# Three pairs of chunks by seven block products in place of two, in a linear-attention and three-gate kernel

## The chip, the cores and the metric

The kernel runs on one core of a Trainium2 chip. The metric is the device time of one execution in microseconds (us), lower is better. TensorE (PE) multiplies matrices and loads its stationary operand by a separate sequence (PEld); VectorE (DVE), ScalarE (ACT) and GpSimd (POOL) work elementwise; SyncE (SP) issues most of the data transfers (DMAs). Each engine works through its instructions in the order in which the program has them, and waits for others by semaphores.

## The reference

Linear attention over batch 8, 8 heads, 576 positions, head size 64, and behind it a layer of three gates whose maximum is taken:

```python
q_s = softmax(q, axis=-1)              # over the 64 of a head
k_s = softmax(k, axis=2)               # over the 576 positions
kv  = einsum('bhsd,bhse->bhde', k_s, v)
x   = einsum('bhsd,bhde->bhse', q_s, kv).transpose(0, 2, 1, 3).reshape(4608, 512)
h   = max(x @ w1, x @ w2, x @ w3)      # 4608 x 768
out = h @ w_out                        # 4608 x 512
```

All inputs of the attention are 32-bit floats; the weights arrive as 64-bit floats. The result is wanted at 32-bit accuracy.

## The kernel before

**Precision.** TensorE's fast format (float32r) doesn't hold a whole 32-bit float. Each operand of a large product is therefore split into a high and a low part, and a product of two blocks is three matmuls: low x high, high x low, high x high. A matmul has 128 x 128 stationary and 128 x 512 moving elements.

**Weights.** The three gate weights come in 18 slices of 512 KB (slice n = 3j+i is weight i, columns 128j to 128j+127), w_out in 6. For each slice VectorE and ScalarE shift, clamp and mask the two words of the 64-bit number (L402 to L411), GpSimd adds them (L415), ScalarE makes the high part (L423) and VectorE or GpSimd the low one (L430). The parts stay on chip as `wh`, `wl` (gates) and `oh`, `ol` (w_out).

**Chunks.** The 4608 rows of x make nine chunks of 512: chunk c < 8 is the first 512 rows of batch c; chunk 8 is the 64 rows left over in each of the 8 batches. Attention runs per batch and pair of heads (n = 4b + g): batches 0 and 1 in a form of their own at the start ("turned"; `q` is their query tile, worked on by ScalarE where n is in `Q_BY_ACT`, L675, otherwise by VectorE and ScalarE, L680 to L701), batches 2 to 7 with the rows of `qt` (max, subtract, exp, sum, scale: L688 to L707; transpose to `tb`, L712; eight small DMAs to `qT`, L725; high and low part, L734 and L737). The product with kv leaves x in PSUM (L799), from which x is split (L807 to L819) for a direct chunk, or copied to `xf` (L822, L824) for a paired one.

**Direct gates.** Chunks 0 to 4: for each of 6 blocks of columns and 3 weights, 4 blocks of the inner dimension x 3 products, 216 matmuls (L894); the maxima go over ScalarE (L903) and VectorE (L906), h is split, and the second product takes 72 matmuls (L941).

**Paired gates.** From `PAIRED` on, two chunks are taken together (class `Duo`). The gate of two chunks is seen as a 2 x 2 block product and computed by seven block products P1 to P7 in place of eight (Strassen's scheme in Winograd's form). There are 9 units u (3 pairs of column blocks x 3 weights) of 7 products of 6 matmuls: 378 in place of 432 (L1103). The x operands `xb0` to `xb6` are made once per pair (L1049 to L1055), the weight blocks come from DRAM into small slots `ws` (L1082). Before the first pair, the stored weight blocks `wd` are prepared: three blocks of each unit are stored as they are, 54 stores of 128 KB (`prepare_weights`, L990), and four sums and differences are computed (`mix_weights`: VectorE adds high and low part, L1001, forms the blocks, L1007, ScalarE and VectorE split them, L1010 and L1013) and stored in two DMAs of 512 KB per unit. Before, the pairs are (5,6) and (7,8).

**Order.** All engines' orders are fixed when the program is built: each piece of work is a `Step` with an engine, a cost, conditions and a rank, and `Streams` places the steps by these. The constants at the top (`AT`, `CHUNK`, `LEFT_AT`, `FIRST_LOADS` and so on) are ranks. SyncE's queue issues in that order too; a DMA whose condition isn't met holds back those behind it. `xb` and `ws` lie where the gate weights lay, so they can't be written until the last direct gates have read them. A condition `before` in `Duo` says so:

```python
before = [("gates", PAIRED - 1), *(("kept", u) for u in range(9))] if c == PAIRED else [("gates", c - 2)]
```

Of the kernel before, what the change touches and what calls it, by code (L numbers as in the profile page):

```python
# [32 lines left out]
EAGER = 0.3  # L33

FIRST, CHUNK, SLICE = 143.0, 39.5, 1.32

AT = (38.7, -49.7, 32.6, 13.7, 143.7, 146.4, 163.0, 85.8)
STEP = (7.87, 0.38)
SLICES_AT, SLICE_STEP, SLICE_HI, SLICE_LO = -59.7, 0.11, 1.39, 0.51
GATES_AT = 1000.0  # L40
FIRST_LOADS = 'vkwkKqvwKVwVqqkwvqkv'
# [4 lines left out]
Q_BY_ACT = (0, 3, 4, 5, 6, 7)  # L46
# [162 lines left out]
def linear_attention_then_maxout_ffn(  # L209
# [133 lines left out]
    def by_f32(n):  # L343
        return X_F32 and n >= TURNED * NP
# [25 lines left out]
    class Slice:  # L370
# [25 lines left out]
        def join(self, room):  # L396
# [28 lines left out]
        def lo(self, room):  # L425
# [4 lines left out]
            unit[e].tensor_sub(out=lo, in0=self.view(self.low.bitcast(F32)), in1=h.bitcast(F32))  # L430
# [942 lines left out]
```

## Time and profile before

| what | value |
|---|---|
| median of 3 runs | 677.64 us (676.85 to 678.12) |
| profiled execution | 678.42 us |
| its span | 676.6 us |
| granted TensorE clock, mean | 0.992 |
| bytes moved by DMA | 107.64 MB |
| matmuls | 3434 |
| largest groups | L894 222.6 us, L1103 173.1 us, L941 59.7 us (one of several forms) |

The span runs from the first to the last recorded instruction; the execution's time is 1.82 us longer. A group's busy time is the sum of its instructions' times, which overlap on TensorE, so groups add to more than the engine's busy time. The profile's waits are idle time of an engine with what ended it.

### The profile page before, as it was taken

To read this page: it belongs to the slowest core of one execution; us is meant where nothing else is said; L and a number is where in the kernel's file an instruction comes from. 1 tells how busy PE (TensorE), PEld (TensorE's weight loads), DVE (VectorE), ACT (ScalarE), POOL (GpSimd) and SP (SyncE) were. 2 spreads that over 40 slices of the span, in tenths; PEclk is the share of its full clock that TensorE was granted. 3 is DMA by queue.
4 is the path that set the end of the run, shared out by engine and by line. 5 is a ranking of instruction groups with operands and counts; after the bars stand their busy time and mean duration, and the time that the engine had idled before them with its cause. 6 is when DMAs were issued, how large, how long until landed. Compare 5 with 4: busy or idle time off the path is not lost.

```text
span 676.6 us, 10151 instructions
## 1 busy us (share of the span) xinstructions
PE 646.9 (96%) x3434; PEld 530.3 (78%) x3434; DVE 463.5 (68%) x893; ACT 293.3 (43%) x660; POOL 61.4 (9%) x75
## 2 busy tenths in 40 slices
PE   2679999999999999999999999999999999999997
PEld 2467787788887888878888888888888788888875
DVE  5679998788707998899998998985525712333521
ACT  5579957433414443444444444644234432123132
POOL 2223232310100001101000001000000000000000
PEclk9979999999999999999999999999999999999999
DMA  9757634365755434554575646876665126766021
GB/s 231 193 159 235 168 95 141 115 173 145 221 173 156 122 89 145 159 179 125 143 211 169 177 132 204 267 221 173 204 191 166 63 89 193 190 197 195 24 63 62
DMA packets 125635, 107.64 MB, mean 159 GB/s; under 512 B 52368, under 2 KB 101008, under 8 KB 125584
## 3 DMA queue, kind: packets, MB, share of 16 engines
q1 hardware_dynamic: 125504, 106.87, 55.1%
q8 instruction: 27, 0.44, 0.3%
q14 instruction: 24, 0.20, 0.1%
q10 hardware_dynamic: 80, 0.13, 0.1%
HBM read 73.92 MB, written 25.95 MB: 148 GB/s over the span
## 4 chain that ended last, share of the span: by engine, by line
PE 87%; SPq 5%; DMA 4%; DVE 2%; issue 1%; ACT 1%; DVEq 0%; ACTq 0%
PE pf L894 34%; PE pf L1103 25%; PE pf L941 20%; DMA wst<-in_moe_w_dram 2%; PE pa L799 2%; PE pa L590 2%; PE sm L799 1%; DMA qt<-in_q_dram 1%; SPq L725 1%; DMA vt<-in_v_dram 1%; SPq L1224 1%; SPq L476 1%; PE sm L633 1%; DVE xb L1051 1%; SPq L1227 0%
## 5 line engine op out<-in xcount | busy, mean ns | idle before, releaser
L894 PE MATMUL pf<-x,wh 128*128 128x512 f32 x720 | 222.6, 390 | 0.0
L1103 PE MATMUL pf<-xb,ws 128*128 128x512 f32 x756 | 173.1, 389 | 0.0
L1103 PEld LDWEIGHTS pf<-xb,ws 128*128 128x128 f32 x756 | 141.6, 188 | 29.3
L894 PEld LDWEIGHTS pf<-x,wh 128*128 128x128 f32 x720 | 135.4, 188 | 27.5 <-issue 0.2
L894 PE MATMUL pf<-x,wl 128*128 128x512 f32 x360 | 143.8, 399 | 1.5 <-ACT m L903 0.9
L894 PEld LDWEIGHTS pf<-x,wl 128*128 128x128 f32 x360 | 67.7, 188 | 16.4 <-ACT m L903 1.3
L1132 DVE TENSOR_TENSOR mm<-pf,mm 128x512 f32<-128x512 f32 x24 | 16.6, 692 | 67.4 <-PE pf L1103 67.3
L941 PE MATMUL pf<-oh,hs 128*128 128x512 f32 x192 | 59.7, 390 | 1.0 <-DVE hs L1187 1.0
L906 DVE TENSOR_TENSOR m<-pf,m 128x512 f32<-128x512 f32 x60 | 41.3, 688 | 11.2 <-PE pf L894 10.4
L941 PE MATMUL pf<-ol,h_h 128*128 128x512 f32 x120 | 48.5, 404 | 0.0
L967 ACT COPY m<-pf 128x512 f32<-128x512 f32 x35 | 20.5, 587 | 63.5 <-PE pf L941 63.1
L560 POOL PARTITION_ALL_REDUCE kma<-km x24 | 21.3, 889 | 287.4 <-DVE km L557 218.1
L941 PE MATMUL pf<-oh,h_l 128*128 128x512 f32 x120 | 46.8, 390 | 0.0
L941 PE MATMUL pf<-oh,h_h 128*128 128x512 f32 x120 | 46.8, 390 | 0.0
L941 PEld LDWEIGHTS pf<-oh,hs 128*128 128x128 f32 x192 | 36.0, 188 | 9.3 <-DVE hs L1187 1.9
L415 POOL TENSOR_TENSOR wst<-wx,wst 128x512 int32<-128x512 int32 x24 | 31.8, 1327 | 87.7 <-DVE wx L411 64.7
L941 PE MATMUL pf<-ol,hs 128*128 128x512 f32 x96 | 37.6, 392 | 0.0
L1187 DVE TENSOR_TENSOR hs<-mm,hs 128x512 fp32r<-128x512 f32 (+1 forms) x32 | 16.7, 555 | 28.1 <-ACT hs L1185 28.1
L1151 ACT COPY pf<-pf 128x512 f32<-128x512 f32 x18 | 10.3, 570 | 57.7 <-PE pf L1103 57.7
L712 DVE STREAM_TRANSPOSE tb<-qt 128x576 f32<-128x576 f32 x24 | 30.6, 1276 | 1.7 <-DMA qT<-tb 1.0
L909 ACT CAST h_h<-m 128x512 fp32r<-128x512 f32 x30 | 18.6, 620 | 29.6 <-DVE m L906 29.6
L941 PEld LDWEIGHTS pf<-ol,h_h 128*128 128x128 f32 x120 | 22.5, 188 | 5.2 <-issue 0.7
(186 smaller groups left out, 936.5 us busy)
## 6 DMA issues: line engine op xcount, KB each, us to landing
ws<-wd SPq DMA_DIRECT2D x126, 256.0 KB, 3.0
wst<-in_moe_w_dram SPq DMA_DIRECT2D x18, 512.0 KB, 4.8
out_dram<-m SPq DMA_DIRECT2D x31, 256.0 KB, 2.8
vt<-in_v_dram SPq DMA_DIRECT2D x56, 128.0 KB, 3.0
qt<-in_q_dram SPq DMA_DIRECT2D x24, 288.0 KB, 3.5
qT<-tb SPq DMA_DIRECT2D x192, 36.0 KB, 1.9
kt<-in_k_dram SPq DMA_DIRECT2D x24, 256.0 KB, 3.2
wd<-mix_h SPq DMA_DIRECT2D x9, 512.0 KB, 3.2
```

The lines of the kernel that those rows point to most:

```text
L415: nc.gpsimd.tensor_add(out=low.bitcast(I32), in0=x.bitcast(I32), in1=low.bitcast(I32))
L560: nc.gpsimd.partition_all_reduce(kma, km, P, bass_isa.ReduceOp.max)
L712: nc.vector.transpose(out=tb.rearrange("p e (c s) -> p s e c", s=QS), in_=self.qt.rearrange("p s (e c) -> p s e c", e=2))
L799: nc.tensor.matmul(out=out, lhsT=l, rhs=r[:, cs], start=(i == 0), stop=(i == last))
L894: nc.tensor.matmul(out=ps, lhsT=l[:, cc, js], rhs=r, start=(cc == 0 and t == 0), stop=(cc == NC - 1 and t == 2))
L906: nc.vector.tensor_max(out=m, in0=self.m.pop((j, i)), in1=m)
L909: nc.scalar.copy(out=h, in_=m)
L941: nc.tensor.matmul(out=po, lhsT=l, rhs=r[:, j, :], start=(j == 0 and i == 0), stop=(j == NJ - 1 and i == 2))
L967: nc.scalar.copy(out=o, in_=po)
L1103: nc.tensor.matmul(out=bank[on], lhsT=w[:, a, k], rhs=x[:, b, k], start=(i == 0 and p in ("P1", "P5")), stop=(i == 5), skip_group_check=True,)
L1132: nc.vector.tensor_max(out=m, in0=bank[on], in1=m)
L1187: nc.vector.tensor_tensor(out=o[:, 1, jj], in0=mm[:, h, jj, ts], in1=o[:, 0, jj].bitcast(F32), op=ALU.subtract)
```

## The change

- `PAIRED` goes from 5 to 3: chunks 0 to 2 are direct, the pairs are (3,4), (5,6), (7,8). First-stage matmuls: 648 direct and 1134 paired in place of 1080 and 756.
- The high and low parts of the weights lie interleaved in `wa`. GpSimd's sum goes to one of four buffers `wf`, and each gate slice is stored from there as it is, as a plain float, to `keep_w` (18 stores of 256 KB during the start). `keep_weights` stores the split weights whole: 12 stores of 768 KB.
- `mix_weights` loads plain blocks from `keep_w` (9 loads of 512 KB) and no longer adds parts; one store of 1 MB per unit to `keep_s`.
- Weight loads of the pairs come from `keep_a` (P1, P4, P2: rows of 512 bytes) and `keep_s` (the other four products: 2 KB); 8 slots `ws` in place of 10; the buffers `s5`, `u2` are single.
- The x operands of the pairs are formed in another order, in place.
- Query work of batches 0 and 1 is on ScalarE for two pairs of heads (4 and 6) instead of six; exponentials of n = 8, 9 and scalings of n = 8 to 12 are done row by row on ScalarE; the main loads of v from batch 2 on are issued by ScalarE (48 DMAs); queries may be loaded earlier.
- The ranks are set anew.

Of the table of ranks two lines are shown.

```diff
-FIRST_LOADS = 'vkwkKqvwKVwVqqkwvqkv'
+FIRST_LOADS = 'vkwkKkqvwwKVVkqqqvwvk'
...
-Q_BY_ACT = (0, 3, 4, 5, 6, 7)
+Q_BY_ACT = (4, 6)
...
+NORM_FROM, NORM_TO = 8, 13
+ROWS_FROM, ROWS_TO = 8, 10
...
-PAIRED = 5
+PAIRED = 3
...
-    wh = [place(f"wh{i}", [P, NC, DF], F32R, W_AT + HALF * i) for i in range(3)]
-    wl = [place(f"wl{i}", [P, NC, DF], F32R, W_AT + HALF * (3 + i)) for i in range(3)]
+    wa = [place(f"wa{i}", [P, NC, 2, DF], F32R, W_AT + DF * NC * 8 * i) for i in range(3)]
+    wh, wl = ([t[:, :, hl, :] for t in wa] for hl in range(2))
...
+    wfs = Placed("wf", [P, CH], F32, SCR_AT, 4)
...
-    ws = [place(f"ws{i}", [P, 2, 2, P], F32R, SCR_AT + 2048 * i if i < 4 else W_AT + 57344 + 2048 * (i - 4)) for i in (0, 1, *range(4, 12))]
...
+    ws = [place(f"ws{i}", [P, 2, 2, P], F32R, W_AT + 57344 + 2048 * i) for i in range(8)]
...
-    wd = [dram.tile([P, 7, 2, 2, P], F32, name=f"wd{u}") for u in range(9)]
+    keep_a = [dram.tile([P, NC, 2, DF], F32, name=f"keep_a{i}") for i in range(3)]
+    keep_w = [dram.tile([P, 2, NC, P], F32, name=f"keep_w{u}") for u in range(9)]
+    keep_s = [dram.tile([P, 2, 2, 2, 2, P], F32, name=f"keep_s{u}") for u in range(9)]
...
+        def keep(self):
+            n = self.n
+            j, i = divmod(n, 3)
+            yield Step("S", 0.64, [("w", n)], gives=("plain", n), kb=256)
+            nc.sync.dma_start(out=keep_w[3 * (j // 2) + i][:, j % 2], in_=self.view(self.w))
...
+                    e = yield Step("S" if self.turned else V_ON, 0.64, [prev], kb=128 if self.turned else 200)
...
+                by_act = ROWS_FROM <= n < ROWS_TO
+                nc.vector.tensor_reduce(out=qm, in_=rows3, op=ALU.max, axis=AX.X, negate=by_act)
+                for s in range(QS if by_act else 0):
+                    if s % 3 == 0:
+                        yield Step("A", 3 * 0.33)
+                    nc.scalar.activation(
+                        out=rows3[:, s, :], in_=rows3[:, s, :], func=AF.Exp, bias=qm[:, s : s + 1],
+                        accum_out=qs[:, s : s + 1],
+                    )
+            if not self.turned and not by_act:
...
+            if NORM_FROM <= n < NORM_TO:
+                for s in range(QS):
+                    if s % 3 == 0:
+                        yield Step("A", 3 * 0.22, gives=("qn", n) if s == 6 else None)
+                    nc.scalar.activation(
+                        out=rows3[:, s, :], in_=rows3[:, s, :], func=AF.Copy, scale=qs[:, s : s + 1]
+                    )
...
-    WINO = {"P1": (0, 0), "P5": (6, 1), "P2": (1, 2), "P6": (3, 3), "P7": (5, 4), "P3": (4, 5), "P4": (2, 6)}
-
-    def prepare_weights():
-        for u in range(9):
-            jp, i = divmod(u, 3)
-            js = slice(2 * jp * P, 2 * (jp + 1) * P)
-            hv, lv = (t[i][:, :, js].rearrange("p c (r n) -> p r c n", r=2) for t in (wh, wl))
-            yield Step("S", 0.64, ["turn", ("split", 6 * jp + i), ("split", 6 * jp + 3 + i)], kb=128)
-            for part, (block, r, cc) in enumerate(((0, 0, 0), (1, 0, 2), (2, 1, 2))):
-                for hl, t in enumerate((hv, lv)):
-                    if part or hl:
-                        yield Step("S", 0.64, kb=128, gives=("kept", u) if part == 2 and hl else None)
-                    nc.sync.dma_start(out=wd[u][:, block, hl], in_=t[:, r, cc : cc + 2].bitcast(F32))
+    WINO = {
+        "P1": ("a", 0, 0), "P5": ("s", 1, 1), "P4": ("a", 1, 1), "P6": ("s", 0, 0), "P2": ("a", 0, 1), "P3": ("s", 0, 1),
+        "P7": ("s", 1, 0),
+    }
+    X_OF = {"P1": 0, "P5": 1, "P6": 2, "P2": 3, "P3": 4, "P7": 5, "P4": 6}
+
+    def keep_weights():
+        last = KEEP_AFTER
+        for i in range(3):
+            for c in range(NC):
+                e = yield Step(
+                    KEEP_ON, 0.64, [last, *(("split", 3 * j + i) for j in range(NJ))], gives=("kept", i, c), kb=768
+                )
+                (nc.sync if e == "S" else nc.scalar).dma_start(out=keep_a[i][:, c], in_=wa[i][:, c].bitcast(F32))
+                last = ("kept", i, c)
+            yield Step("-", 0.0, [last], gives=("kept", i))
...
-            for r in range(2):
-                yield Step("V", dve(CH), ["turn", "left", ("split", 6 * jp + i), ("split", 6 * jp + 3 + i)], port="V")
-                nc.vector.tensor_tensor(out=v[:, r], in0=hv[:, r].bitcast(F32), in1=lv[:, r].bitcast(F32), op=ALU.add)
+            yield Step("S", 0.64, ["left", ("plain", 6 * (u // 3) + u % 3), ("plain", 6 * (u // 3) + 3 + u % 3), ("low_mix", u - 1) if u else None], kb=512)
+            nc.sync.dma_start(out=v, in_=keep_w[u])
...
+            yield Step("S", 0.64, kb=1024, gives=("mixed", u))
+            nc.sync.dma_start(
+                out=keep_s[u].rearrange("p r c k t n -> p (r c k t n)"), in_=mix.rearrange("p r c t n -> p (r c t n)")
+            )
...
+                jp, i = divmod(u, 3)
+                kind, r, cc = WINO[p]
+                slot = ws[(at + n) % len(ws)].bitcast(F32)
+                after = [("kept", i) if kind == "a" else ("mixed", u)]
+                if c == PAIRED and n < len(ws):
+                    after.append(("gates", c - 1))
+                    after += [("kept", v) for v in range(3)]
                 yield Step("S", 0.64, after, take=[("ws", (c, p, u))], gives=("w", c, p, u), kb=256)
-                nc.sync.dma_start(out=ws[slot].bitcast(F32), in_=wd[u][:, WINO[p][0]])
+                if kind == "a":
+                    js = slice((2 * jp + r) * P, (2 * jp + r + 1) * P)
+                    nc.sync.dma_start(
+                        out=slot.rearrange("p k t n -> p (k t) n"),
+                        in_=keep_a[i][:, 2 * cc : 2 * cc + 2, :, js].rearrange("p k t n -> p (k t) n"),
+                    )
+                else:
+                    nc.sync.dma_start(
+                        out=slot.rearrange("p k t n -> p (k t n)"),
+                        in_=keep_s[u][:, r, cc].rearrange("p k t n -> p (k t n)"),
+                    )
```

**TensorE, at the beginning of the first pair.** Before, the end of the second product of chunk 2 (L941; `ol`, `oh` are w_out, `h_h5` the sixth block of h) and the gates of chunk 3 behind it:

```order
L941 MATMUL pf_3685<-ol_106,h_h5_91 128x512
L941 MATMUL pf_3685<-oh_105,h_h5_91 128x512
L941 MATMUL pf_3685<-oh_105,h_l5_97 128x512
L894 MATMUL pf_3729<-x0_84,wl0_81 128x512
L894 MATMUL pf_3729<-x0_84,wh0_78 128x512 x2
```

The same place in the changed program (the second product is now L984, the paired products L1163):

```order
L984 MATMUL pf_3150<-ol_103,h_h5_88 128x512
L984 MATMUL pf_3150<-oh_102,h_h5_88 128x512
L984 MATMUL pf_3150<-oh_102,h_l5_94 128x512
L1163 MATMUL pf_3182<-xb0_114,ws0_121 128x512 x6
L1163 MATMUL pf_3195<-xb1_115,ws1_122 128x512 x6
L1163 MATMUL pf_3207<-xb2_116,ws2_123 128x512 x6
```

P1 of the first pair (operand `xb0`) stands where the direct gate of chunk 3 began, and P5 (`xb1`) six matmuls later.

**VectorE, at the making of the first pair's operands.** Before, the first two conversions, for pair (5,6), between attention of later batches:

```order
L712 STREAM_TRANSPOSE tb_4307<-qt_4169 128x9x64
L906 TENSOR_TENSOR m_4266<-pf_4292,m_4266 128x512
L555 TENSOR_TENSOR kh_4325<-kt1_149 128x256
L556 TENSOR_TENSOR km_4326<-kh_4325 128x128
L557 TENSOR_TENSOR km_4326<-km_4326,kt1_149 128x128
L1051 TENSOR_TENSOR xb0_111<-xf0_107,xb0_111 128x1024
L1051 TENSOR_TENSOR xb2_113<-xf0_107,xb2_113 128x1024
```

In the changed program, for pair (3,4) (L1097 is the split, L1101 a sum of blocks, L1059 the low part of mixed weights):

```order
L1059 TENSOR_TENSOR mix_1456<-bdf_166,mix_1456 128x4x128
L780 TENSOR_TENSOR q_l_3054<-qT_2927,q_h_3035 128x576
L1059 TENSOR_TENSOR mix_1456<-bdf_166,mix_1456 128x4x128
L755 STREAM_TRANSPOSE tb_112<-qt1_111 128x9x64
L737 TENSOR_REDUCE qs9_238<-qt0_110 128x9
L594 TENSOR_TENSOR ke_3090<-kt0_159,kma_2970 128x2x5x64
L1101 TENSOR_TENSOR xf1_105<-xf1_105,xf0_104 128x1024
L1097 TENSOR_TENSOR xb4_118<-xf1_105,xb4_118 128x1024
L739 TENSOR_SCALAR qs9_238<-qs9_238 128x9
L740 RECIPROCAL qs9_238<-qs9_238 128x9
L1101 TENSOR_TENSOR xf1_105<-xf1_105 128x1024
L1097 TENSOR_TENSOR xb1_115<-xf1_105,xb1_115 128x1024
```

Mixing of weights and attention of a later batch now stand among the conversions. Four splits and two sums stand ahead of TensorE's P5, up to its operand `xb1` in the last row (those for `xb0` and `xb3` are just above this piece).

**SyncE, first loads of weight blocks.** Before, at the beginning of pair (5,6):

```order
L1082 DMA ws0_118<-wd1_136 128x512
L479 DMA kt1_149<-in_k_dram 128x2x256
L1082 DMA ws1_119<-wd1_136 128x512
L481 DMA kt1_149<-in_k_dram 64x2x64
L1082 DMA ws4_120<-wd1_136 128x512
L1082 DMA ws5_121<-wd2_137 128x512
```

In the changed program, at the beginning of pair (3,4):

```order
L1139 DMA ws4_125<-keep_s1_147 128x512
L539 DMA qt0_110<-in_q_dram 128x576
L1134 DMA ws5_126<-keep_a2_136 128x4x128
L1063 DMA keep_s5_151<-mix_1456 128x2048
L1047 DMA bdf_166<-keep_w6_143 128x1024
L1139 DMA ws6_127<-keep_s2_148 128x512
```

The store of the sixth unit's mixed weights (`keep_s5`) and the plain load of the seventh (`keep_w6`) now stand among the loads of the pair that uses them.

More of the change, by code (lines that the diff above doesn't have):

```diff
@@ L343, in by_f32 @@
     def by_f32(n):
-        return X_F32 and n >= TURNED * NP
+        return F32_FROM <= n < F32_TO
     def main_rows(src, b, hs):
@@ L429, in lo, with wf_free @@
             h, lo = self.parts()
-            unit[e].tensor_sub(out=lo, in0=self.view(self.low.bitcast(F32)), in1=h.bitcast(F32))
+            unit[e].tensor_sub(out=lo, in0=self.view(self.w), in1=h.bitcast(F32))
+        def keep(self):
[3 more added lines that the diff above has]
+            nc.sync.dma_start(out=keep_w[3 * (j // 2) + i][:, j % 2], in_=self.view(self.w))
+        def wf_free(self):
+            yield Step("-", 0.0, [("plain", self.n), ("split", self.n)], free=[("wf", self.n)])
     def x_free(b):
@@ L705, in q_steps @@
             which, cost = ("VG", (dve(rows * D), pool(rows * D))) if self.turned else ("V", dve(rows * D))
-            e = yield Step(which, cost, gives=("qn", n), port=which)
-            unit[e].tensor_tensor(out=rows3, in0=rows3, in1=qs.unsqueeze(2).broadcast_to([P, rows, D]), op=ALU.mult)
+            if NORM_FROM <= n < NORM_TO:
[5 more added lines that the diff above has]
+                    )
+            else:
+                e = yield Step(which, cost, gives=("qn", n), port=which)
+                unit[e].tensor_tensor(out=rows3, in0=rows3, in1=qs.unsqueeze(2).broadcast_to([P, rows, D]), op=ALU.mult)
             if self.turned:
@@ L717, in q_steps @@
                     end = i == P // BL - 1 and e == 1
-                    yield Step(
-                        "S", 0.6, take=[("qT", n)] if i == e == 0 else (), free=[("tb", n)] if end else (),
+                    eng = yield Step(
+                        TB_ON, 0.6, ["turn"], take=[("qT", n)] if i == e == 0 else (), free=[("tb", n)] if end else (),
                         gives=("qhl" if by_f32(n) else "qT", n) if end else None, kb=36,
@@ L1040, in convert, with split @@
             c = self.c
-            before = [("gates", PAIRED - 1), *(("kept", u) for u in range(9))] if c == PAIRED else [("gates", c - 2)]
+            before = [("gates", c - 2)]
+            if c == PAIRED:
+                before = [("gates", c - 1), *(("kept", i) for i in range(3))]
             (x0, e0), (x1, e1) = self.x(0), self.x(1)
             b11, b21, b12, b22 = x0[:, 0:2], x0[:, 2:4], x1[:, 0:2], x1[:, 2:4]
-            spare = bdf.rearrange("p n c -> p (n c)").rearrange("p (k t) -> p k t", k=2)
-            mixed = [("mixed", 8)] if c == PAIRED else [("cv", c - 2, 6)]
-            def split(i, src, after, gives):
+            def split(i, src, after):
                 yield Step("A", act(2 * CH), [*before, *after])
@@ L1103, in products @@
                     nc.tensor.matmul(
-                        out=bank[on], lhsT=w[:, a, k], rhs=x[:, b, k], start=(i == 0 and p in ("P1", "P5")), stop=(i == 5),
+                        out=bank[on], lhsT=w[:, k, a], rhs=x[:, b, k], start=(i == 0 and p in ("P1", "P5")), stop=(i == 5),
                         skip_group_check=True,
@@ L1153, in ago @@
             def ago(what):
-                return (what, c, u - 2) if u >= 2 else None
+                return (what, c, u - 1) if u else None
             def met():
```

114 lines of the change are left out of this document (58 added, 56 removed).

## Prediction

> **What bounds the kernel now.** I read the page first: the counts, the 40 slices, and the line that divides the chain of work that ended last.
>
> ```profile
> PE 646.9 (96%) x3434; PEld 530.3 (78%) x3434; DVE 463.5 (68%) x893; ACT 293.3 (43%) x660; POOL 61.4 (9%) x75
> PE   2679999999999999999999999999999999999997
> DVE  5679998788707998899998998985525712333521
> PE 87%; SPq 5%; DMA 4%; DVE 2%; issue 1%; ACT 1%; DVEq 0%; ACTq 0%
> ```
>
> TensorE is busy for 96% of the span and holds 87% of the chain; only its first slices and the last one have holes. VectorE is the second engine: nearly full from the 4th slice to the 27th (51 to 457 us) but for the 12th, and half idle or more later. Next I cut the span into stages. The columns are the window, its length, the busy time of PE, PEld, DVE, ACT and POOL with the instructions, the granted clock, the DMA share and GB/s.
>
> ```profile
> 0.00:47.00 47.00, 24.50 (x145) 19.10 (x145) 29.85 (x80) 27.37 (x84) 12.36 (x17) 0.89 0.73 196
> 36.40:41.90 5.50, 5.50 (x24) 5.05 (x25) 3.19 (x11) 3.21 (x18) 1.29 (x1) 0.50 0.60 194
> 47.00:111.00 64.00, 63.34 (x367) 49.25 (x367) 58.16 (x120) 50.26 (x149) 19.86 (x15) 1.00 0.56 163
> 111.00:130.00 19.00, 19.00 (x85) 15.01 (x84) 14.41 (x26) 11.17 (x23) 7.52 (x18) 1.00 0.28 87
> 47.00:185.00 138.00, 137.34 (x766) 109.93 (x766) 118.68 (x237) 82.93 (x214) 33.34 (x40) 1.00 0.56 162
> 185.00:205.00 20.00, 20.00 (x90) 16.56 (x89) 1.56 (x3) 2.97 (x5) 0.00 (x0) 1.00 0.63 187
> 205.00:280.00 75.00, 74.11 (x451) 61.68 (x450) 66.53 (x139) 32.02 (x69) 5.51 (x7) 1.00 0.49 133
> 205.00:410.00 205.00, 203.80 (x1211) 169.39 (x1210) 188.61 (x383) 91.36 (x193) 12.73 (x15) 1.00 0.53 150
> 429.00:520.00 91.00, 91.00 (x446) 75.70 (x445) 54.51 (x90) 33.65 (x68) 0.70 (x1) 1.00 0.70 202
> ```
>
> From 47 us on TensorE hardly waits: 0.66 us of 138, 1.2 of 205, none in the first pair (429 to 520). The start loses 47.00 - 24.50 = 22.5 us. So matmuls that go away anywhere after 47 us come off the end one for one, unless another engine then falls behind.
>
> **The matmuls taken out.** Chunks 3 and 4 become a pair: 378 first-stage matmuls in place of 2 x 216, so 54 fewer. Their price is the distance between two starts, not the 390 ns that each lasts, since they overlap. The chain has it:
>
> ```profile
> 130.22 14.28 PE pf L894 x63
> 238.41 0.13 PE pa L799
> 239.20 1.39 PE pf L894 x6
> 279.46 2.57 PE pf L894 x12
> 553.53 84.32 PE pf L1103 x372
> ```
>
> 84.32/372 = 226.7 ns in a pair, 14.28/63 = 226.7 in the direct gates: both kinds run at one rate, and 54 x 226.7 ns = 12.2 us. Second products and attention matmuls keep their number. Term: -12.2.
>
> **Work that changes on VectorE.** The two directions have to be added up, because this engine must have the new first pair's operands ready 150 us sooner.
>
> ```profile
> L680 DVE TENSOR_TENSOR qe<-q,qm 128x512 f32<-128x512 f32 x1 | 0.7, 684 | 0.0
> L701 DVE TENSOR_REDUCE qs<-qe 128x8 f32<-128x512 f32 x1 | 0.7, 677 | 0.0
> L404 DVE TENSOR_SCALAR wx<-wst 128x512 uint32<-128x512 uint32 x5 | 2.2, 445 | 10.8 <-DMA wst<-in_moe_w_dram 10.8
> L1001 DVE TENSOR_TENSOR bdf<-wh,wl 128x512 f32<-128x512 f32 x18 | 12.3, 703 | 0.0
> L1007 DVE TENSOR_TENSOR bdf<-bdf 128x256 f32<-128x256 f32 x36 | 14.9, 414 | 0.2
> L1013 DVE TENSOR_TENSOR mix_l<-bdf,mix_h 128x512 fp32r<-128x512 f32 x18 | 12.4, 691 | 0.0
> L1051 DVE TENSOR_TENSOR xb<-xf,xb 128x1024 fp32r<-128x1024 f32 x8 | 9.7, 1245 | 0.0
> L1055 DVE TENSOR_TENSOR bdf<-xf 128x1024 f32<-128x1024 f32 x2 | 2.4, 1221 | 0.0
> L712 DVE STREAM_TRANSPOSE tb<-qt 128x576 f32<-128x576 f32 x24 | 30.6, 1276 | 1.7 <-DMA qT<-tb 1.0 <-DMA ws<-wd 0.4
> L675 ACT ACTIVATE qe<-q,qm 128x64 f32<-128x64 f32 x48 | 16.1, 338 | 0.8 <-PE pa L747 0.7
> ```
>
> Added at the start: five q subtractions (L680) and four q sums (L701) that were on ScalarE, and five more absolute values of weights (L404): 3.4 + 2.7 + 2.2 = 8.3 us, less copies that go to ScalarE. Removed: the 18 additions of weight parts (L1001), 12.3 us, since the plain sum is now loaded. Added: one more pair's conversion, seven splits (L1051) and four sums (L1055), 13.6 us, while two chunks lose the max, split and copy work of direct gates and gain that of pairs, which is about even. Net, VectorE has about as much as before, and 463.5 of 665 us is no bound over the whole.
>
> Where it matters is the moment when the first pair begins. In the new order its P1 stands right behind the second product of chunk 2, where before chunk 3's direct gates began (279.46 in the chain). Against the instructions that VectorE had begun by 280 us before, the new order puts ahead of the operand of P5 (the second product): 12 more small sums of mixed weights (L1007, 5.0 us) and 8 more differences (L1013, 5.5), less four additions (2.8); four splits and two sums of the conversion (7.4); the nine q steps of the start (6.2) and the absolute values (2.5 with smaller ones), less copies (2.6); and attention of later batches that now stands earlier, three transposes (L712, 3.8) with the k, q and x steps around them (7.6 net): 32.6 us of durations. Durations overlap a little: what had run by 280 us adds to 240.9 us, while the windows have 29.85 + 118.68 + 1.56 + 66.53 = 216.6 busy, so 32.6 x 0.90 = 29.3, and VectorE needs 216.6 + 29.3 = 245.9 us of work by then.
>
> TensorE arrives at P5 at 279.5, plus 3.2 (four blocks of chunk 4's x, 0.79 each, from 238.41 to 239.20), plus six matmuls (1.4), less the 0.9 us below: 283.2. VectorE may thus idle 37.3 us until then. Before, it idled 63.4 by 280, of which 18.44 in the hole from 185 to 205, which the next row explains:
>
> ```profile
> DVE kh L555 <- DMA kt<-in_k_dram: 19.2, 3, 17.7
> 184.13 0.49 SPq L990 DMA_DIRECT2D wd<-wh  x1
> PE pf L894 <- ACT m L903: 0.9, 1, 0.9
> 130.91 0.76 DVE L688 TENSOR_REDUCE qm<-qt 128x9 f32<-128x576 f32 x1 [3.32 <-DMA qt<-in_q_dram]
> ```
>
> SyncE's queue issues 54 stores of 128 KB (L990) in one run up to 197 us and chunk 3's k loads stand behind them. They leave, 12 stores of 768 KB take their place: 42 issues fewer there, while the whole change has 18 plain stores and 9 plain loads more and 9 stores of mixed weights fewer on the queue. The stores of mixed weights wait for ScalarE and VectorE, and behind each stand loads of weights that don't need it. Without that hole VectorE idled 45.0 us, which would make it 7.7 late; if it fills the 3.3 us wait for qt and keeps the rest of the later rate (16.4 of 205 us idle), it idles 17.15 until 47 us, 5.84 + 4.59 - 3.3 = 7.1 until 130, and 8% of the 153 us to P5, 12.2: 36.5, in time. Ends 0 and 7.7; I take 2, nearer to the low one because a late VectorE idles less. Term: +2. The hole also cost TensorE one wait of 0.9 us. Term: -0.9.
>
> **ScalarE.** It loses 32 q exponentials of the start (L675, 338 ns) and gains 18 of later rows and 45 scalings of such rows, 63 x 0.34 = 21 less 11 us, and 48 issues of V loads at the 0.6 us that one takes on SyncE (row 197.40 below), 29 us. It is 43% busy, and with 40 us more of 665 it stays at half: cost 0, hidden beside TensorE's products. If that cover fails, an issue stands ahead of a copy that frees a bank, 0.6 us each time.
>
> **The start.** TensorE's 22.5 us there are waits for first loads, one above all:
>
> ```profile
> 30.44 4.70 DMA wst<-in_moe_w_dram
> 36.36 0.59 PE L760 MATMUL pf<-of_head,qf 128*128 128x2 f32 x2 [5.67 <-ACT qf L751]
> ```
>
> The third and later weight loads move among the other loads: by the order of SyncE's queue 7.70 MB stand ahead of the fifth weight load in place of 6.65. At 196 GB/s that is 5.4 us later, the upper end. The lower end is that the new order closes most of the 5.67 us hole, and the half-speed stretch behind it (5.5 us at clock 0.50, so 2.75 lost): -4. New plain stores (18 of 256 KB) and V loads on ScalarE's queue lie among these. I take 0, since nothing in the rows favours one end. [...]
>
> **The first pair's transfers.** Loads per pair stay 63 of 256 KB, now from two places, half of them in shorter runs of bytes, and with 8 places for them to land instead of 10.
>
> ```profile
> ws<-wd SPq DMA_DIRECT2D x126, 256.0 KB, 3.0
> wd<-mix_l SPq DMA_DIRECT2D x9, 512.0 KB, 4.4
> wd<-wh SPq DMA_DIRECT2D x27, 128.0 KB, 2.0
> qT<-tb SPq DMA_DIRECT2D x192, 36.0 KB, 1.9
> 197.40 0.59 SPq L725
> ```
>
> Eight places are 8 x 6 x 226.7 ns = 10.9 us of products ahead, against 3.0 us to land, so that costs nothing in a quiet stage. The first pair is not quiet: chunk 5's and 6's attention, mixed weights that aren't done yet (stores of 1 MB, loads of 512 KB) and the 63 loads come together. From the order I count 136 SyncE DMAs with 28.0 MB, and 1.3 MB of V on ScalarE's queue, from the end of chunk 2's gates to the last product of the pair: 72 + 378 matmuls, 102 us. The old first pair moved 202 x 91 us = 18.4 MB in its window. SyncE needs 136 x 0.6 = 82 us of the 102. The rate must be 29.3/102 = 287 GB/s. The start moved 196 at a share of 0.73, so 268 at a full share and 109 us, 7 too many; the old first pair 202 at 0.70, 289 at full share, without a wait of TensorE. Ends 0 and 7; I take 1, as loads of mixed weights can slip past the products that need them first.
>
> ```profile
> PE pf L941 <- DVE hs L1187: 1.0, 1, 1.0
> ```
>
> A third pair's second product waits for VectorE's split as the two did (1.0 us over both): +0.5.
>
> **Sum.** Span 676.6 - 12.2 - 0.9 + 0 + 2 + 1 + 0.5 = 667.0. The profiled execution took 678.42 with that span; the median is 677.64, 1.04 above the span, so 668.0 us.
>
> **Rivals.** *VectorE late.* The 45.0 us of idle time return, and TensorE waits 7.7 at P5 in place of 2: 673.7. For it: VectorE was 92% busy from 205 to 410 us (188.61 of 205). Against it: it waited on transfers whose queue is now shorter. [...]
>
> *The transfers bound the first pair.* One mechanism: loads of weights, kept within 8 places, run at the rate of the mixed traffic. At the 268 of the start, the gain survives; below 29.3/(102 + 9.3) = 263 GB/s in this stretch it is gone. At 240 GB/s the pair takes 122 us, 20 more instead of 1: 687. For it: none of the long windows above moved more than 202 GB/s. Against it: windows that moved less were not asked for more, and the old pairs never starved.
>
> *A better start.* If the fifth weight load's hole closes and TensorE stays at full clock: 668.0 - 4 to -7: 661 to 664. The new list of first loads would have to do it with more bytes ahead.
>
> **How the numbers follow.** Few waits, my sum with its small ends (664 to 672): 0.54. VectorE late, without the clock: 0.15; with it 0.06. Transfers: 0.16. Better start: 0.09. Faster takes the first, the last and nearly all of the second, 0.76; same 0.07; slower 0.17. The range reaches from 661 to 677 and leaves out the transfers and little else; the likeliest case's own is 664 to 672.
>
> **What would show it.** PE with 3380 matmuls, and L894's distance unchanged. No run of small stores near 190 us and no VectorE hole of 18 us there. VectorE at most 2 us late at the first P5 near 283 us. In the first pair, waits of the products for `ws` loads of 1 us in all: many of them, with a DMA share near 1, prove the transfers' rival. The prediction is wrong if TensorE's idle time after 47 us grows from 7 to over 10 us, or if the start's 22.5 us change by more than 4.

## The result: 25 us slower, and the profile after

The changed kernel takes 702.7 us (median of 4 runs, 699.24 to 706.03), the kernel before 677.25 beside it (676.59 to 678.12): a ratio of 1.0375, 95% interval 1.0322 to 1.0427. 668.0 had been forecast, within 661 to 677. From the page of the changed kernel: the counts, the slices of TensorE, its granted clock (PEclk) and the DMA share, and the line that divides the chain:

```profile
PE 646.5 (92%) x3380; PEld 522.1 (74%) x3380; DVE 480.7 (69%) x892; ACT 317.1 (45%) x711; POOL 62.2 (9%) x76
PE   2769999999999869979988899999999999999997
PEclk9969999999999989989999999999999999999999
DMA  9859663477678766868979884276666216666221
PE 58%; DMA 16%; DVE 15%; SPq 5%; issue 3%; ACT 2%; ACTq 0%; DVEq 0%
```

The 54 matmuls are gone (3434 to 3380), yet TensorE is busy as long as before (646.5 us, 646.9 before), and the chain has 31% on transfers and VectorE in place of 6%. Cut at the first product of the first stage that differs (before: chunk 3's direct gates, after: P1 of the first pair) and at the first product of pair (5,6), first before and then after; columns as in the prediction:

```profile
0.00:279.30 279.30, 255.26 (x1444) 206.68 (x1445) 215.92 (x456) 144.60 (x369) 51.20 (x64) 0.98 0.58 162
279.30:428.70 149.40, 149.09 (x883) 123.78 (x882) 137.95 (x267) 68.94 (x141) 9.46 (x10) 1.00 0.58 171
428.70:676.60 247.90, 242.51 (x1109) 199.79 (x1108) 109.59 (x173) 79.77 (x151) 0.70 (x1) 1.00 0.52 149
```

```profile
0.00:303.30 303.30, 266.45 (x1543) 211.80 (x1544) 260.14 (x514) 170.54 (x425) 55.17 (x67) 0.97 0.71 214
303.30:454.50 151.20, 137.62 (x732) 110.47 (x731) 118.99 (x222) 69.76 (x140) 7.02 (x9) 0.97 0.73 227
454.50:701.40 246.90, 242.42 (x1109) 199.78 (x1107) 101.55 (x158) 76.75 (x146) 0.00 (x0) 1.00 0.49 149
253.50:260.30 6.80, 5.55 (x16) 4.68 (x17) 6.18 (x13) 2.54 (x6) 0.70 (x1) 0.50 0.83 271
308.10:314.90 6.80, 4.17 (x10) 3.31 (x11) 4.31 (x6) 4.88 (x10) 0.00 (x0) 0.50 0.70 220
355.90:359.30 3.40, 3.23 (x8) 2.03 (x8) 3.40 (x6) 2.20 (x5) 0.00 (x0) 0.50 0.88 276
```

From pair (5,6) on nothing is lost (246.9 against 247.9). Ahead of P1 stand 98 more attention matmuls (some 1543 against 1444: three x blocks at 0.79 us, 80 matmuls of kv at 1.32 us for 40), 5.0 us; so P1 was due at 284.3 and came at 303.3: 19.0 late. The stage behind was due to take 149.4 - 12.2 - 5.0 = 132.2 and took 151.2: 19.0 again. 19.0 + 19.0 - 12.2 - 1.0 = 24.8, the difference of the spans. Of the first 19.0, 12.8 us are waits of TensorE (36.85 idle against 24.04); of the second, 13.3. Most of the rest is the clock: it stood at 0.50 for 6.8, 6.8 and 3.4 us at the three places above, and 3.4 us longer than before at the start. By an estimate half of the time in which TensorE works in such a stretch is lost: at the three places it works for 5.55, 4.17 and 3.23 us, so some 6.5. TensorE's idle time after 47 us, which the prediction named as its sign, grew from 7.2 to 31.9 us.

TensorE's main waits behind the start, and SyncE's longest wait for a landing (us in total, times, longest):

```profile
PE pa L842 <- DVE q_l L780: 11.7, 6, 5.8
PE pf L1163 <- ACT pf L1211: 4.6, 1, 4.6
PE pf L1163 <- DMA ws<-keep_a: 2.9, 2, 1.5
PE pf L1163 <- DMA ws<-keep_s: 1.8, 1, 1.8
SPq L768 <- DMA vt<-in_v_dram: 15.1, 7, 5.2
```

The waits name VectorE first. The chain of the longest of them, ahead of 254.75 us, says what VectorE itself waited for (start, length, what; `...` stands for lines left out):

```profile
239.83 7.86 DMA vt<-in_v_dram
...
247.70 0.51 SPq L768
...
249.53 1.84 DMA qT<-tb
...
251.47 0.61 ACT q_h L777
...
253.95 0.76 DVE q_l L780
...
254.75 0.61 PE pa L842
```

A queries' transfer (qT) was issued late, because SyncE's issue waited for a v load; x needs it, and TensorE needs x. The 4.6 us wait in the first pair ends in the same way: a v load takes 8.61 us to land (from 295.63), the qT behind it lands at 307.9, and the copy of a PSUM bank (`pf`) stands in ScalarE's order behind the work on that qT. Landing times between 205 and 300 us, first before, then after (KB each, median us):

```profile
qT<-tb SPq DMA_DIRECT2D x56, 36.0 KB, 1.9
vt<-in_v_dram SPq DMA_DIRECT2D x17, 128.0 KB, 2.9
```

```profile
qT<-tb SPq DMA_DIRECT2D x50, 36.0 KB, 3.1
bdf<-keep_w SPq DMA_DIRECT2D x5, 512.0 KB, 6.4
vt<-in_v_dram ACTq DMA_DIRECT2D x13, 128.0 KB, 5.5
```

### The profile page after: what moved, and what is told of

Read it like the earlier page. It is cut to its first block, busy times and chain, and to the rows that moved or that the text cites. A ratio compares the mean times of both kernels' runs of the same rounds, so it can differ in the third digit from the quotient of the medians.

```text
span 701.4 us, 10268 instructions
## 1 busy us (share of the span) xinstructions
PE 646.5 (92%) x3380; PEld 522.1 (74%) x3380; DVE 480.7 (69%) x892; ACT 317.1 (45%) x711; POOL 62.2 (9%) x76
## 4 chain that ended last, share of the span: by engine, by line
PE 58%; DMA 16%; DVE 15%; SPq 5%; issue 3%; ACT 2%; ACTq 0%; DVEq 0%
PE pf L1163 32%; PE pf L984 16%; PE pf L937 6%; DMA vt<-in_v_dram 6%; SPq L768 3%; DMA wst<-in_moe_w_dram 3%; DMA qT<-tb 3%; PE pa L842 2%; DMA ws<-keep_a 2%; DMA qt<-in_q_dram 1%; DVE tb L755 1%; DVE wx L425 1%; DVE wx L420 1%; DVE m L949 1%; DVE wx L421 1%
## 5 line engine op out<-in xcount | busy, mean ns | idle before, releaser
L1163 PE MATMUL pf<-xb,ws 128*128 128x512 f32 x1134 | 266.8, 394 | 10.7 <-ACT pf L1211 4.6
L1163 PEld LDWEIGHTS pf<-xb,ws 128*128 128x128 f32 x1134 | 213.7, 190 | 58.8 <-ACT pf L1211 5.0
L937 PE MATMUL pf<-x,wa 128*128 128x512 f32 x648 | 161.9, 403 | 0.0
L937 PEld LDWEIGHTS pf<-x,wa 128*128 128x128 f32 x648 | 121.9, 192 | 27.3 <-issue 1.9
L984 PE MATMUL pf<-oh,hs 128*128 128x512 f32 x288 | 89.3, 390 | 0.0
L1192 DVE TENSOR_TENSOR mm<-pf,mm 128x512 f32<-128x512 f32 x36 | 24.8, 689 | 71.1 <-PE pf L1163 71.1
L984 PEld LDWEIGHTS pf<-oh,hs 128*128 128x128 f32 x288 | 54.1, 188 | 11.9 <-DVE hs L1247 0.9
L984 PE MATMUL pf<-ol,hs 128*128 128x512 f32 x144 | 56.5, 392 | 0.0
L434 POOL TENSOR_TENSOR wf<-wx,wst 128x512 int32<-128x512 int32 x18 | 26.1, 1458 | 70.1 <-DVE wx L425 27.6
L984 PEld LDWEIGHTS pf<-ol,hs 128*128 128x128 f32 x144 | 27.0, 188 | 6.0 <-ACT hs L1245 0.5
L984 PE MATMUL pf<-ol,h_h 128*128 128x512 f32 x72 | 28.9, 401 | 0.0
L984 PE MATMUL pf<-oh,h_l 128*128 128x512 f32 x72 | 28.1, 390 | 0.0
L984 PE MATMUL pf<-oh,h_h 128*128 128x512 f32 x72 | 28.1, 390 | 0.0
L1245 ACT CAST hs<-mm 128x512 fp32r<-128x512 f32 (+1 forms) x48 | 23.3, 515 | 8.9 <-DVE mm L1199 8.9
L1097 DVE TENSOR_TENSOR xb<-xf,xb 128x1024 fp32r<-128x1024 f32 x18 | 21.7, 1217 | 6.7 <-ACT xb L1095 6.7
```

Source lines behind the costliest of these rows:

```text
L434: nc.gpsimd.tensor_add(out=self.w.bitcast(I32), in0=x.bitcast(I32), in1=low.bitcast(I32))
L937: nc.tensor.matmul(out=ps, lhsT=l[:, cc, js], rhs=r, start=(cc == 0 and t == 0), stop=(cc == NC - 1 and t == 2))
L984: nc.tensor.matmul(out=po, lhsT=l, rhs=r[:, j, :], start=(j == 0 and i == 0), stop=(j == NJ - 1 and i == 2))
L1097: nc.vector.tensor_tensor(out=xb[i][:, 1], in0=src, in1=xb[i][:, 0].bitcast(F32), op=ALU.subtract)
L1163: nc.tensor.matmul(out=bank[on], lhsT=w[:, k, a], rhs=x[:, b, k], start=(i == 0 and p in ("P1", "P5")), stop=(i == 5), skip_group_check=True,)
L1192: nc.vector.tensor_max(out=m, in0=bank[on], in1=m)
```

## The experiments

P1 and "stage" are the two cuts above: the start of the first pair's first product, and from there to the first product of pair (5,6). Due are 284.3 and 132.2. Both columns are of one profiled execution each; the four executions of the changed kernel lie 6.8 us apart, so a difference of some 3 us in these columns says little.

| kernel | time, us | ratio to before, 95% | P1 | stage |
|---|---|---|---|---|
| changed | 702.7 | 1.032 to 1.043 | 303.3 | 151.2 |
| e1 v loads issued by SyncE | 701.6 | 1.034 to 1.040 | 302.2 | 150.6 |
| e4 no plain transfers | 681.7 | 1.004 to 1.008 | 285.8 | 145.4 |
| e5 plain transfers, 1/8 of bytes | 684.1 | 1.007 to 1.013 | 292.8 | 142.9 |
| e6 plain stores without wait | 705.9 | 1.039 to 1.043 | 303.2 | 152.0 |
| e9 plain loads, 1/8 of bytes | 687.6 | 1.011 to 1.017 | 294.8 | 143.3 |
| e10 weight loads, 1/8 of bytes | 693.6 | 1.020 to 1.025 | 300.6 | 143.7 |
| e11 e4 without mixing | 685.2 | 1.006 to 1.014 | 289.2 | 147.3 |
| e12 without mixing | 704.2 | 1.036 to 1.041 | 303.4 | 152.4 |
| e13 bulk issued by ScalarE | 691.8 | 1.017 to 1.025 | 303.1 | 139.6 |
| e14 bulk issued by GpSimd | 701.9 | 1.032 to 1.038 | 302.1 | 149.8 |
| e15 qT issued by ScalarE | 693.3 | 1.019 to 1.024 | 301.6 | 143.0 |
| e16 bulk, plain stores by GpSimd, v by SyncE | 707.7 | 1.039 to 1.046 | 304.4 | 156.3 |

**The v loads (e1, e2).**

```diff
-                    (nc.sync if e == "S" else nc.scalar).dma_start(out=self.vt[...
+                    nc.sync.dma_start(out=self.vt[...
```

> The changed kernel with one word changed: the 48 main loads of v from batch 2 on are issued by SyncE instead of ScalarE, at the place where they stand in the common order; TensorE's, VectorE's and ScalarE's other work keeps its order. Theory A (SyncE and ScalarE hold each other up: every DMA waits for the one eight places before it in the common order, whichever queue issued it; v loads issued late by a busy ScalarE hold back SyncE's small qT transfers, these q_l and x): TensorE's 11.7 us of waits for q_l fall under 4, the half-speed stretches behind them go, 680 to 690 us. Theory B (the bytes: a DMA share of 0.8 and more from 250 to 410 us) : the bytes stay, so within 5 of 702.7. Theory C (VectorE has too much ahead of the first pair): within 5 of 702.7 as well.

e2 sets `V_ON = 'S'` and lets the order be planned anew.

> The changed kernel with V_ON = 'S': as the run before, but the order of all engines is planned anew with v on SyncE. Theory A: as far as the new order is no worse, 675 to 690. Theories B and C: 698 to 708.

701.6 and 705.6 us. In e1 no qT issue of SyncE waits for a v landing any more (15.1 us in the changed kernel), and the time stayed. The chain of e1 at the place shown above:

```profile
239.05 8.54 DMA keep_a<-wa
...
248.18 0.59 SPq L768
...
253.50 0.75 DVE q_l L780
```

The last qT issue of this group comes at 248.18 us in place of 248.90, and q_l at 253.50 in place of 253.95: SyncE now has the v loads' issues to make, and the landing ahead is that of a 768 KB store. The wait that the chain showed first was not what set the pace. Theory A's cure, v on SyncE, fell; that small issues stand behind other landings did not, as the store took the place of the v load. In e2, whose order differs, TensorE stands 15.3 us for the first pair's first weights.

**Two pairs only (e3), and the old kernel with three (e8).** e3 is the changed kernel with `PAIRED = 5`; e8 is the kernel before with

```diff
-LEFT_AT, PREP_AT, PREP_STEP = 230.0, 280.0, 0.5
-PAIRED = 5
+LEFT_AT, PREP_AT, PREP_STEP = 150.0, 200.0, 0.5
+PAIRED = 3
...
-            before = [("gates", PAIRED - 1), *(("kept", u) ...
+            before = [("gates", PAIRED - 1), ("mixed", 8), *(("kept", u) ...
```

> The changed kernel with PAIRED = 5: chunks 3 and 4 direct again, two pairs, all other parts of the change kept (v on ScalarE, plain stores, split weights stored whole, ranks). 54 matmuls more than the changed kernel, 12.2 us. Theory A: the small qT transfers are late as well, 695 to 710, TensorE's waits for q_l over 8 us. Theory B: the 63 loads of the first pair come when little else moves, 677 to 685. Theory C: VectorE has 130 us more until the first pair: 677 to 685, with waits for q_l that go too.

> The kernel before with PAIRED = 3 and the little that this needs (the left queries and the mixing of weights 80 ranks sooner, the first pair's operands after the last mixed weight): a third pair without plain stores, whole stores, new places and new ranks. If the third pair as such is what costs (it starts before VectorE and the loads can serve it): 695 or more, with TensorE waiting ahead of the first pair. If the other parts cost: 672 to 682.

e3: 690.2 us (ratio 1.017 to 1.020), outside what any of the three theories gave. Without a third pair the change is slower too, by 12.7 us: TensorE idles 34.4 us until 300 us, 24.4 before, and from there to pair (5,6) not at all. The second stage of the start (47 to 130 us), before and in e3:

```profile
47.00:130.00 83.00, 82.34 (x450) 64.27 (x450) 72.58 (x144) 61.42 (x171) 27.39 (x33) 1.00 0.49 146
```

```profile
47.00:130.00 83.00, 76.72 (x404) 57.75 (x405) 79.90 (x147) 62.02 (x176) 28.14 (x19) 1.00 0.59 188
```

e8: 716.1 us (1.054 to 1.058). With the old transfers the third pair is worse: TensorE stands ahead of it for x and then for its first weights (timeline of PE, idle time and releaser in brackets):

```profile
301.25 0.61 PE L799 MATMUL pa<-q_l,bdh 128*128 128x288 f32 x1 [8.85 <-DVE q_l L737]
324.55 2.90 PE L1103 MATMUL pf<-xb,ws 128*128 128x512 f32 x6 [11.32 <-DMA ws<-wd]
```

With the other parts of the change the third pair takes 702.7 us, without them 716.1; e8 has only the few ranks changed that it needs, so a better order for it isn't excluded. Beside e3, the third pair adds 12.5 us (702.7 against 690.2), where its 54 matmuls fewer should have saved 12.2.

**The plain transfers (e4, e5, e6, e9).** e4 omits both DMAs; e5 keeps them at an eighth:

```diff
-            nc.sync.dma_start(out=keep_w[...][:, j % 2], in_=self.view(self.w))
+            nc.sync.dma_start(out=keep_w[...][0:16, j % 2], in_=self.view(self.w)[0:16])
...
-            nc.sync.dma_start(out=v, in_=keep_w[u])
+            nc.sync.dma_start(out=v[0:16], in_=keep_w[u][0:16])
```

e6 stores a constant (`in_=ident...broadcast_to([P, NC, P])`), so that no store waits for GpSimd's sum; e9 makes the loads alone small.

> The changed kernel without the 18 plain stores and the 9 plain loads (the mixed weights are then made of stale values): 9.4 MB and 27 DMAs fewer, most of the loads between 180 and 370 us; all other instructions in the same order. Theory A: a little, 694 to 702. Theory B: 4.7 MB less of reads at about 260 GB/s in the busy stretch, 18 us of transfer: 680 to 692. Theory C: within 3 of 702.7.

> The changed kernel with the 18 plain stores and 9 plain loads kept in place, each with 16 of 128 partitions, an eighth of its bytes (the mixed weights are then wrong): same DMAs, same waits, same order, 8.3 MB less. Theory B1 (bytes): as without them, 680 to 685. Theory B2 (SyncE stands at a plain store until GpSimd's sum is there, and what is behind it is late): waits of SyncE for wf stay near 12 us, 697 to 703. Theory B3 (27 more places in the turn of the DMAs in flight): 695 to 703.

> The changed kernel with the 18 plain stores taking their bytes from a constant tile instead of GpSimd's sum (the mixed weights are then wrong): same bytes, same places, but no store waits for GpSimd, and GpSimd never for a store. Theory B1: 698 to 705. Theory B2: the 12 us of SyncE's waits go, 684 to 692. Theory B3: 698 to 705.

> The changed kernel with the 9 plain loads at an eighth of their bytes (mixed weights wrong), the 18 plain stores whole: 4.1 MB less, nearly all of it after 180 us. By bytes alone half of what small stores and loads gave together (18.6 of 702.7): 691 to 696, with the second product of chunk 1 as late as in the changed kernel (197 us), since only stores stand before it. If the loads matter because VectorE and ScalarE stand in order behind a late load: 684 to 690.

681.7, 684.1, 705.9 and 687.6 us. With order, DMA count and conditions the same, 8.3 MB fewer of 136 give 18.6 us; the 4.1 MB of the loads alone give 15.1, more than their half. That is the time forecast for VectorE and ScalarE standing behind a late load; e12 below excludes it, since nothing there reads what the loads bring, and the time stays. In e4, P1 comes at 285.8, 1.5 from due: the plain transfers are nearly the whole of the loss ahead of the first pair, and 6 (e4) to 8 us (e5) of the loss within it. Theory B2 (SyncE held up by GpSimd) fell with e6, B3 (their number) with e5, though e5's P1 is 7.0 later than e4's. Landing times between 205 and 300 us, e4, then e5:

```profile
qT<-tb SPq DMA_DIRECT2D x53, 36.0 KB, 3.0
vt<-in_v_dram ACTq DMA_DIRECT2D x16, 128.0 KB, 3.8
```

```profile
qT<-tb SPq DMA_DIRECT2D x55, 36.0 KB, 2.8
vt<-in_v_dram ACTq DMA_DIRECT2D x16, 128.0 KB, 4.1
```

The landing of qT hardly falls (3.1 in the changed kernel), though 19 to 21 us are gone; that of v does (5.5). Nor do SyncE's waits for landings follow the time: between 130 and 420 us they add to 36.3 us in the changed kernel, 10.4 in e1 at 701.6 us and 31.7 in e4 at 681.7.

**VectorE's arithmetic (e11, e12).** Both store zeros as mixed weights (e11 on top of e4) and leave out

```diff
-                nc.vector.tensor_tensor(out=o, in0=x, in1=y, op=op)
...
-                nc.scalar.copy(out=mix[:, r, :, 0, :].bitcast(F32R), in_=v[:, r])
...
-                nc.vector.tensor_tensor(out=mix[:, r, :, 1, :].bitcast(F32R), in0=v[:, r], ...
```

> The changed kernel without plain stores and loads and without the arithmetic of mixing (36 sums and 18 differences on VectorE, 27 us, 18 casts on ScalarE); zeros are stored as mixed weights. If VectorE's work is the rest of the loss (681.7 us without plain transfers, against 668): 666 to 672. If it is not: 678 to 682.

> The changed kernel without the arithmetic of mixing, all transfers in place (zeros are stored as mixed weights). If bytes alone hold it up: 697 to 703. If VectorE is as much to blame as the bytes: 680 to 690.

685.2 and 704.2 us: no gain, with the transfers or without. The first two stages of e12:

```profile
0.00:303.40 303.40, 265.14 (x1543) 211.36 (x1544) 249.32 (x484) 165.08 (x415) 56.84 (x68) 0.97 0.70 214
303.40:455.80 152.40, 137.31 (x732) 110.01 (x731) 109.69 (x199) 65.73 (x132) 7.02 (x9) 0.98 0.72 224
```

VectorE works 10.8 us less ahead of P1 than in the changed kernel (260.14), and P1 comes at the same time. In the changed kernel VectorE has the operand of P5 ready at 299.1 us, before TensorE begins P1: the work of VectorE that TensorE waits for is q_l, ahead of that.

**The weight loads of the first pair (e7, e10).** e10 brings 16 of 128 rows from the ninth load on (`out=slot[:rows]`); e7 brought 32 rows and took only those into the products (`lhsT=w[:rows, k, a], rhs=x[:rows, b, k]`).

> The changed kernel with the 63 weight loads of the first pair bringing 32 of 128 partitions (and its products summing over those 32 alone): same DMAs, waits and matmuls, 12.4 MB less between 285 and 415 us. Theory B1: the first pair's stage, 151 us from its first product to the next pair's first, falls to 137 to 140, the time to 686 to 692. Theory B3 or waits of another kind: stage 147 to 152, 698 to 703. If VectorE is what is late there: 147 to 152 too.

> The changed kernel with the first pair's weight loads from the ninth on bringing 16 of 128 partitions (its products take old weights in the other rows, all 128 rows are used): same DMAs, waits and matmuls, 12.6 MB less from 303 to 415 us. By bytes: the stage from the first pair's first product to the next pair's falls from 151 to 137 to 142, the time to 688 to 694. If VectorE or the number of DMAs holds the stage: 148 to 152, 699 to 703.

e10: 693.6 us, the stage 7.5 us shorter, its rate down to

```profile
300.60:444.30 143.70, 135.31 (x732) 109.49 (x732) 119.64 (x222) 69.98 (x140) 7.01 (x9) 0.99 0.50 152
```

The weight loads' bytes give 7.5 of the stage's 19.0. e7 measured something else: 768.3 us, with a granted clock of 0.50 from 320 to 480 us (last section), so it says nothing on bytes.

**Which queue (e13 to e16).** With all bytes kept, e13 turns `nc.sync` into `nc.scalar`, e14 into `nc.gpsimd`, at the 30 stores of split weights, plain loads and stores of mixed weights; e15 turns it into `nc.scalar` at the qT transfers; e16 adds the plain stores to e14 and v to SyncE.

> The changed kernel with the 30 bulk transfers that are new in kind (12 stores of split weights of 768 KB, 9 plain loads of 512 KB, 9 stores of mixed weights of 1 MB) issued by ScalarE in place of SyncE, at the same places in the common order; all bytes stay, TensorE's, VectorE's and GpSimd's order too. Theory F (first in, first out: the small chained transfers q, qT, k of SyncE's queue wait behind bulk in the same queue): the median landing of qT between 205 and 300 us falls from 3.1 to under 2.4 us, 685 to 693. Theory T (the transfer engines are shared by all queues, and it is the total at that moment): qT's landing stays near 3, 698 to 706. ScalarE waiting for a mixed weight's store speaks in both for some us more.

> As the run before, but the 30 bulk transfers are issued by GpSimd, which has little else to do after 130 us. Theory F: 682 to 692, qT's landing under 2.4 us. Theory T: 698 to 706.

> The changed kernel with the 192 small qT transfers (36 KB) issued by ScalarE, at the same places; all bulk stays on SyncE. Theory F: their landing falls to about 2 us, but ScalarE issues 192 x 0.55 us more and waits for tb: 690 to 700. Theory T: landing near 3 and the same issue time: 703 to 715.

> The changed kernel with the 30 bulk transfers and the 18 plain stores issued by GpSimd, and the v loads by SyncE: the version nearest to a cure if the queue is what costs. Theory F: 672 to 685. Theory T: 695 to 705.

691.8, 701.9, 693.3 and 707.7 us. qT's landing did not fall below 3.0 us in any (205 to 300 us; e13, then e15):

```profile
qT<-tb SPq DMA_DIRECT2D x53, 36.0 KB, 3.7
```

```profile
qT<-tb ACTq DMA_DIRECT2D x54, 36.0 KB, 3.6
```

For the landing, theory T's forecast came in these four runs: with the same bytes moved, qT took 3.0 to 3.7 us, against 3.1 in the changed kernel, whichever queue had it or the bulk. In time, taking work off SyncE and giving it to ScalarE gave 9 to 11 us, in the first pair nearly alone (139.6 and 143.0 in place of 151.2, with no wait for `ws` in e13): the times that theory F forecast, without its cause. On GpSimd it gave nothing; the chain of e14 around one of TensorE's new waits:

```profile
312.84 0.51 POOL keep_s L1063
313.36 7.47 issue
320.85 0.56 POOL bdf L1047
321.43 0.67 POOL kma L587
322.13 0.83 DVE kep L594
```

The plain load comes 7.47 us after the issue of the store ahead of it, time for which the profile shows no releaser (such stores took 6.0 us to land, median, between 300 and 400 us), and the maximum over k (`kma`), which attention needs, stands behind it on GpSimd.

**Two attempts at a cure (e17, e18).** The first units are mixed from the parts on chip, with the bulk on ScalarE; e18 is that with two pairs and no plain transfer.

```diff
+            if u < FROM_CHIP:                    # 5 in e17, 9 in e18
+                for r in range(2):
+                    yield Step("V", dve(CH), ["left", ("split", 6 * jp + i), ...
+                    nc.vector.tensor_tensor(out=v[:, r], in0=hv[:, r]..., in1=lv[:, r]..., op=ALU.add)
+            else:                                # store, load and condition as before
```

> The changed kernel with the bulk transfers issued by ScalarE (as in e13) and the first five of the nine units mixed from the parts on chip: VectorE adds high and low part, 10 more sums of 0.70 us, and 10 plain stores and 5 plain loads go, 5.2 MB; the order is planned anew. If bytes ahead of and in the first pair are what costs, and VectorE's arithmetic isn't: 677 to 686, against 691.8 for e13. If VectorE's sums cost after all: 690 to 700.

> As e17 but with PAIRED = 5 and all nine units mixed on chip, so no plain transfer at all: two pairs, 9.4 MB fewer than e3 (690.2). If bytes are what made e3 slower than the kernel before: 676 to 682. If the new start and ranks did: 686 to 691.

709.5 (1.040 to 1.048) and 692.0 us (1.017 to 1.023). In e17 ScalarE stands at a plain load until the store before it has landed, and the copy of a PSUM bank (u) that TensorE needs stands behind it:

```profile
310.49 8.16 DMA keep_s<-mix
318.67 0.33 ACTq L1061
...
320.02 0.50 ACT u L1220
320.56 5.60 PE pf L1179 x16
```

e17 missed both of its forecasts. e18 has no plain transfers and is no better than e3, which speaks against these bytes as what costs the two-pair form its 12 us. It doesn't settle that: its order is another, and TensorE idles 26.0 us until 47 us in it, 23.7 in e3. No version that computes the whole came under the kernel before.

## Why the prediction was wrong, step by step

- *54 matmuls, -12.2.* Right as far as it shows: 3380 matmuls, and pair (5,6) takes 123.5 us to the next one (454.5 to 578.0), 124.7 before (428.7 to 553.4): one rate. What it saves is smaller than the waits on top of it.
- *The hole at 185 to 205 us, -0.9.* Right: neither the wait for `m` nor the 18 us hole of VectorE is left (it is busy for 19.62 of the 20 us).
- *The start, 0 (-4 to 5.4).* Too low. TensorE idles 0.5 us more until 47, 3.6 more from there to 130, and the clock stands at 0.50 for 13.6 us in place of 10.2: about 6. Most of it goes with the plain stores: by 130 us TensorE has begun 568 matmuls in the changed kernel and 590 in e4, 22 more, by an estimate 5 us at 227 ns each. I had named these stores and given them no price.
- *VectorE's lag, +2 (0 to 7.7).* This step failed, in mechanism and size: P1 was 19.0 late, start included, and not for VectorE's work. I added up VectorE's instructions and asked when it would be done. It had more to do than I summed (255.9 us of busy time up to P5's operand, not 245.9), yet TensorE didn't wait at P5, and e12 takes 10.8 us of work away for nothing. I gave the bytes ahead of P1 a price only at the fifth weight load; 214 GB/s moved there in place of 162. e5 shows what some of them cost: with the plain transfers at an eighth, P1 is 10.5 earlier at the same order and count. (I also took four blocks of x ahead of P1, 3.2 us; it was three and 80 matmuls of kv, 5.0, which come off the later stage.)
- *The first pair's transfers, +1 (0 to 7).* Mis-sized: 19.0. The mean rate was no measure: the whole stage moved 227 GB/s, under the 289 that I called free. e5 gives 8.3 us of it to the plain transfers, e10 7.5 to the weight loads, e13 11.6 to what moves with the bulk to another queue; they overlap.
- *The clock.* The sum had no term for new stretches at half speed, only a chance of 0.06 for a late VectorE with the clock; no run shows which waits bring one. What the runs showed in its place: the wait of 5.75 us came with 6.8 us at 0.50 with 5.55 of work in it, so 2.8 more by the estimate above, the wait of 4.59 us with 6.8 us at 0.50 with 4.17 of work, and a third stretch of 3.4 us, with 3.23 of work, came behind waits of 1.34 and 1.82 us.
- *The rivals.* The transfers' rival was nearest (687, chance 0.16): right in kind, but I gave it only the stage of the first pair, and half of the loss stood ahead of that.

Shown is that the plain transfers' bytes cost 18.6 us, at fixed order, count and conditions, and that SyncE's waits for GpSimd's sums, the arithmetic of mixing and v's queue do not. Open is how the bytes reach TensorE: the chains lead over late landings to SyncE's issues, but neither qT's landing nor SyncE's waits for landings follow the time from run to run. e13 and e15 give 10 us back without a better landing; I take SyncE's issue order for that part, which is argued, not shown, and e1 speaks against it, where 48 more issues on SyncE cost nothing. What in the new start costs the two-pair form 12 us was not tried piece by piece, nor were e4, e10 and e13 put together.

## What to carry to other kernels

In this kernel, whose engines all run fixed orders, transfers off the critical path were not free: 8.3 MB of 136 cost 18.6 us, and neither the mean rate nor the median landing of the small transfers beside them showed that price. A wait names the last link, and when it is taken away the next one may stand at the same time (e1); shrink the bytes of a transfer, or leave out an engine's arithmetic, with everything else in place, to see which one carries the time. Look at the granted clock behind each new wait of TensorE: here waits of 4.59 and 5.75 us each came with a stretch of 6.8 us at 0.50, which began before the wait ended (at 308.1 and 253.5 us).

## What the runs showed of the hardware that I had not expected

In e7 TensorE was busy without a gap for 160 us at a granted clock of 0.50. The first pair's products use 32 of 128 rows there (window 320 to 480 us, and the groups with 128 and 32 rows):

```profile
320.00:480.00 160.00, 160.00 (x483) 121.06 (x483) 74.16 (x142) 38.08 (x78) 4.65 (x7) 0.50 0.33 100
L1166 PE MATMUL pf<-xb,ws 128*128 128x512 f32 x756 | 173.1, 389 | 0.0
L1166 PE MATMUL pf<-xb,ws 32*128 32x512 f32 x378 | 161.0, 615 | 0.9 <-ACT pf L1214 0.9
```

A matmul with 32 rows lasts 615 ns, one with 128 rows of the later pairs 389 in the same run, at a clock of 1.00 from 500 to 700 us. TensorE's one wait ahead of a product with 32 rows was of 0.9 us. Full clock came back at about 482 us, by an estimate from the mean of 0.68 between 450 and 500 us, when second products with 128 rows had begun (479.41). In the changed kernel, whose first pair uses all 128 rows, that pair's stage has a mean clock of 0.97. Why the clock stayed at 0.50 is not shown: one kernel has it, and nothing in it was varied. The second surprise: a plain load of 64 KB in e5 took 5.2 us to land (median) between 205 and 300 us, little less than one of 512 KB in the changed kernel (6.4). What held it was not tried by itself.
